# Splitting four halves of weights in a group's step, where eight were split

## The chip, the core and the metric

The kernel runs on one core of a Trainium2 chip. A core has a matrix engine (TensorE, PE in the rows, its weight loads PEld), VectorE (DVE), ScalarE (ACT), GpSimd (POOL) and SyncE (SP, which here only issues DMAs). Each engine works through its own list of instructions in the order of the program, and semaphores tell it when an input is there. The metric is the device time of one execution in microseconds (us), the median of several. Before the change it is 1352.58 us (three runs, 1352.49 to 1353.43).

## The reference

Three layers follow each other: a linear attention with gates, a feed-forward layer whose activation is a quotient of polynomials, and a mixture of four experts in which every token goes through every expert.

```
f = 1 / (1 + exp(-f_logit))
for t in range(S):                                   # S = 768, heads 8, batch 4, head size 48
    state = f[t, :, None] * state + outer(k[t], v[t])
    y[t] = q[t] @ state
x = y as 3072 tokens x 384
h = x @ w_in                                          # 384 -> 2048
g = (a0 + a1 h + a2 h^2 + a3 h^3) / (1 + |b0||h| + |b1| h^2 + 1e-6)
x = g @ w_out                                         # 2048 -> 384
for e in range(4):                                    # 384 -> 1024 -> 384
    out += p[:, e] * (relu(x @ w1[e]) @ w2[e])
```

## The kernel before

The 3072 tokens are six groups of 512 (four batches of 128 tokens). Three pipelines run over the groups at the same time and are woven into one list of steps, numbered v here and in the code (L1089): the attention of a later group, the first feed-forward layer of the next group, and the experts of the present group. `product_order` (L366) says which products a step holds. `in2` and `out2` are the two products of the experts for one slot of 128 hidden units, `in1` is the first product of the feed-forward layer, and `out1` is its second product for four slots at once. Products are computed from weights in two parts (a high part and the rest that it leaves), so `in1`, `in2` and `out2` are nine matmuls of 512 columns each and `out1` is 36. The steps 16, 20, 24 and 29 hold an `out1` and are called groups' steps.

A slot's weights are two halves (`halves`, L392). In the order of their use the halves are numbered k = 0, 1, 2, ... The first time that a half is used (96 of them, all within the steps -1 to 31) it goes through three stages. `make_ready` (L813) issues its load into one of NRAW = 8 places of a raw buffer. `split_to` (L832) splits it: ScalarE rounds it to the high part (L837, called a cast below) and GpSimd subtracts that from the raw values (L838, called a split). `store_all` sends both parts to memory, from where the later uses load them. A tile of the ring of R = 14 holds the two parts.

Who calls these sets the order of the engines' work. `take` (L847) gives a product its halves. After each product `emit` asks `make_ready` to load up to 14 halves ahead of the use. At a step's end (L1185) up to four halves are split, up to AHEAD = 8 ahead of the use. Where all eight raw places are taken, `make_ready` itself splits the oldest half until one is free (L822), in the middle of the step.

The other work that matters here, by line:

- `gate_in` and `gate_step`: the activation of the feed-forward layer. ScalarE copies the product (L947) and computes from it (L951, L952, L953, L968, L969, L978), VectorE multiplies (L962, L964 or L971, L967, L976, L986, L988, L993). One such unit is begun and one is finished in a step, and a step's L978 waits for its L976 and L969.
- `relu` (L1001 on ScalarE, L1002 on VectorE) empties the bank of an `in2`.
- `evac1`: after an `out1` its three banks are emptied, by ScalarE copies (L1058) in step 16 itself, by VectorE additions (L1060) in the steps 21, 25 and 29. `evac2` empties the banks of an expert (L1036 on VectorE, L1043 on GpSimd).
- the attention: GpSimd multiplies keys (L453) and queries (L468) by the gates' products, and TensorE's scores (L472) wait for the queries. L447 and L448 (ScalarE) and L459 and L463 (VectorE) make the factor of the queries; L426 is the exponential of the gates, whose logits are loaded as f. L492 and L548 (ScalarE), L553 and L567 (VectorE) and L568 (GpSimd) are the end of a block.

## Time and profile before

| | |
|---|---|
| median of three runs | 1352.58 us |
| profiled execution | 1352.66 us |
| its span, first to last instruction | 1350.9 us |
| TensorE busy | 1324.0 us, 98% |
| VectorE busy | 896.5 us, 66% |
| ScalarE busy | 666.5 us, 49% |
| GpSimd busy | 306.5 us, 23% |
| mean granted clock of TensorE | 0.995 |

The profiled execution is 1.8 us longer than its span. A row of the timeline gives the start in us from the span's start, the time from the first to the last of the merged instructions, the engine, the line, the operation, what it writes and reads, the number of instructions, and in brackets how long the engine sat idle before and what ended that. The granted clock is a share of TensorE's 2.4 GHz.

### The profile page before, as it was taken

Reading aid. Unit: us, or ns where it says so; the run is one execution under the profiler, and the core shown is the slowest. Engines: PE = TensorE matmul, PEld = TensorE weight load, DVE = VectorE, ACT = ScalarE, POOL = GpSimd, SP = SyncE. Lnnn points to the kernel's source line nnn. Section 1 sums busy time; section 2 is a strip of 40 time slices with the busy share of each in tenths; the row PEclk is TensorE's granted clock in tenths of the full one; section 3 lists DMA queues with packets and bytes.
Section 4 is the critical chain, followed back from the end, with each engine's and each line's share of the span. In section 5 each row is a group of like instructions: output and inputs, shape, how many; then the busy total and the mean of one; then the engine's idle time right before and its main releaser. Section 6 shows DMA issues by size and latency. Waiting matters only on the chain.

```text
span 1350.9 us, 19646 instructions
## 1 busy us (share of the span) xinstructions
PE 1324.0 (98%) x7180; PEld 1059.8 (78%) x7180; DVE 896.5 (66%) x1361; ACT 666.5 (49%) x1164; POOL 306.5 (23%) x263
## 2 busy tenths in 40 slices
PE   8998999999999999999999999999999999999998
PEld 7444888777788888888888888888888888888887
DVE  8999658998657666757666847676766465752221
ACT  5986458667344545445445525454535544531111
POOL 2334655676410122110120211010210010110010
PEclk9999999999999999999999999999999999999999
DMA  9537887677875676676666657665757666667660
GB/s 347 210 143 279 280 275 241 239 258 269 292 265 161 213 214 191 185 232 214 213 195 187 212 176 264 216 199 186 220 179 240 194 193 195 191 195 241 191 195 27
DMA packets 115705, 291.03 MB, mean 215 GB/s; under 512 B 13104, under 2 KB 28816, under 8 KB 114832
## 3 DMA queue, kind: packets, MB, share of 16 engines
q1 hardware_dynamic: 115168, 289.56, 66.6%
q8 instruction: 59, 0.97, 0.3%
q14 instruction: 46, 0.38, 0.1%
q10 hardware_dynamic: 432, 0.13, 0.0%
HBM read 240.83 MB, written 48.81 MB: 214 GB/s over the span
## 4 chain that ended last, share of the span: by engine, by line


## 5 line engine op out<-in xcount | busy, mean ns | idle before, releaser
L881 PE MATMUL bank<-x,w 128*128 128x512 f32 x2448 | 593.4, 391 | 3.1 <-DVE gl L1002 3.1
L881 PEld LDWEIGHTS bank<-x,w 128*128 128x128 f32 x2448 | 457.4, 188 | 99.7 <-DVE gl L1002 3.9
L891 PE MATMUL bank<-gh,w 128*128 128x512 f32 x1584 | 494.9, 394 | 3.6 <-DVE s L1060 2.6
L891 PEld LDWEIGHTS bank<-gh,w 128*128 128x128 f32 x1584 | 295.4, 189 | 69.7 <-ACT gh L978 4.4
L891 PE MATMUL bank<-gl,w 128*128 128x512 f32 x792 | 309.7, 391 | 0.0
L1002 DVE SCALAR_TENSOR_TENSOR gl<-bank,gh 128x512 fp32r<-128x512 f32 x192 | 131.5, 685 | 151.8 <-ACT gh L1001 151.5
L1043 POOL TENSOR_TENSOR o<-o,t 128x512 f32<-128x512 f32 x64 | 92.4, 1470 | 523.0 <-DVE t L1036 523.0
L1001 ACT ACTIVATE gh<-bank 128x512 fp32r<-128x512 f32 x192 | 113.9, 594 | 128.9 <-PE bank L881 128.9
L891 PEld LDWEIGHTS bank<-gl,w 128*128 128x128 f32 x792 | 149.4, 189 | 31.5
L967 DVE SCALAR_TENSOR_TENSOR q<-q,sc,r 128x512 f32<-128x512 f32 x80 | 64.8, 810 | 142.1 <-ACT r L952 142.1
L978 ACT CAST gh<-q 128x512 fp32r<-128x512 f32 x80 | 49.2, 615 | 162.9 <-DVE q L976 162.8
L838 POOL TENSOR_TENSOR w<-rawbuf,w 128x384 fp32r<-128x384 f32 x96 | 108.2, 1153 | 79.9 <-ACT w L837 64.3
L947 ACT COPY h<-bank 128x512 f32<-128x512 f32 x80 | 47.0, 588 | 113.6 <-PE bank L881 113.4
L993 DVE TENSOR_TENSOR gl<-q,gh 128x512 fp32r<-128x512 f32 x80 | 57.0, 713 | 32.8 <-ACT gh L978 32.6
L988 DVE SCALAR_TENSOR_TENSOR y<-y,sc,h 128x512 f32<-128x512 f32 x80 | 74.1, 927 | 2.8
L962 DVE SCALAR_TENSOR_TENSOR q<-q,r 128x512 f32<-128x512 f32 x80 | 72.6, 907 | 0.1
L968 ACT ACTIVATE r<-q,sc 128x512 f32<-128x512 f32 x80 | 58.0, 725 | 27.6 <-DVE q L967 20.5
L453 POOL TENSOR_TENSOR k<-k,g 112x512 f32<-112x512 f32 x23 | 34.1, 1484 | 144.7 <-DVE g L439 81.5
L953 ACT ACTIVATE y<-h,sc 128x512 f32<-128x512 f32 x80 | 64.1, 802 | 0.0
L976 DVE SCALAR_TENSOR_TENSOR q<-y,sc,q 128x512 f32<-128x512 f32 x80 | 62.2, 777 | 1.8
L969 ACT ACTIVATE r<-r 128x512 f32<-128x512 f32 x96 | 60.7, 632 | 3.0
L1060 DVE TENSOR_TENSOR s<-s,bank 128x512 f32<-128x512 f32 x45 | 30.0, 684 | 46.1 <-PE bank L891 46.0
(116 smaller groups left out, 1261.6 us busy)
## 6 DMA issues: line engine op xcount, KB each, us to landing
w<-ws SPq DMA_DIRECT2D x448, 384.0 KB, 3.6
ws<-w SPq DMA_DIRECT2D x96, 384.0 KB, 4.4
raw<-in_w_dram SPq DMA_DIRECT2D x16, 768.0 KB, 6.7
rawbuf<-in_w_dram SPq DMA_DIRECT2D x64, 192.0 KB, 4.2
v<-in_v_dram SPq DMA_DIRECT2D x24, 320.0 KB, 5.0
f<-in_qkf_dram SPq DMA_DIRECT2D x24, 256.0 KB, 3.6
k<-in_qkf_dram SPq DMA_DIRECT2D x24, 256.0 KB, 4.0
q<-in_qkf_dram SPq DMA_DIRECT2D x24, 256.0 KB, 4.3
```

The lines of the kernel that those rows point to most:

```text
L838: nc.gpsimd.tensor_tensor(out=t[:, 1], in0=r, in1=t[:, 0].bitcast(F32), op=ALU.subtract)
L881: nc.tensor.matmul(ps, a[:, o], b[:, kk, :], start=(n == 0), stop=(n == 8))
L891: nc.tensor.matmul(acc[m], a[:, o], b, start=(start and n == 0), stop=(stop and n == last))
L953: nc.scalar.activation(out=y, in_=h, func=AF.Identity, scale=sc[:, 0:1], bias=sc[:, 1:2])
L962: vec.scalar_tensor_tensor(out=q0, in0=q0, scalar=QC, in1=r0, op0=ALU.add, op1=ALU.mult)
L967: vec.scalar_tensor_tensor(out=q, in0=q, scalar=sc[:, 5:6], in1=r, op0=ALU.mult, op1=ALU.add)
L969: nc.scalar.activation(out=r, in_=r, func=AF.Exp, scale=-1.0)
L976: vec.scalar_tensor_tensor(out=q0, in0=y0, scalar=sc[:, 3:4], in1=q0, op0=ALU.subtract, op1=ALU.mult)
L988: vec.scalar_tensor_tensor(out=y, in0=y, scalar=sc[:, 2:3], in1=h, op0=ALU.subtract, op1=ALU.mult)
L1001: nc.scalar.activation(out=gh, in_=h, func=AF.Relu)
L1002: nc.vector.scalar_tensor_tensor(out=gl, in0=h, scalar=0.0, in1=gh.bitcast(F32), op0=ALU.max, op1=ALU.subtract)
L1043: add()
```

## The change

`make_ready` no longer splits a half to get room. Where the next half would need a raw place and all eight are taken, it stops, and the half is loaded later: a new call at each step's end, after the splits, goes on with the loads. `take` is made safe for a half that has not been loaded.

```
     def make_ready(n):
         while state["ready"] < min(n, len(uses)):
             k = state["ready"]
+            if first_use[k] and len(raw_of) >= NRAW:
+                break
             state["ready"] += 1
...
                     rawbuf.append(x2p.tile([128, NRAW, DM], F32, tag="x2", name="rawbuf"))
-                while len(raw_of) >= NRAW:
-                    split_to(state["split"] + 1)
                 r = raw_of[k] = rawbuf[0][:, len(seen) % NRAW]
...
     def take(n):
         k = state["used"]
-        split_to(k + n)
+        while state["split"] < k + n:
+            make_ready(state["split"] + 1)
+            split_to(state["split"] + 1)
         state["used"] += n
...
         if v >= -1:
             split_to(min(state["used"] + AHEAD, state["split"] + 4))
+            make_ready(state["used"] + R)
         att.loads(v)
```

The number of splits, their operands and all matmuls stay as they are; the lists of TensorE and of VectorE keep their order. What moves stands in the lists of ScalarE, GpSimd and SyncE. Counted from the code, the halves split in a step were 8 in each of the steps 16, 20 and 24, 2 in the steps 17, 21, 22 and 25, and 3 in the steps 18, 19, 23 and 26. They are now 4 in each of the steps 16 to 22 and 24 to 26, and 3 in the steps 23 and 27. In the steps -1 and 10 to 15 the number stays, but one split leaves the middle of the step for its end.

The first place is GpSimd at the steps -1 to 1. `w_1063`, `w_1065` and `w_1180` are the halves 6, 7 and 8, `k_1136` and `q_1138` the keys and queries of one block of the attention. Before:

```order
L468 TENSOR_TENSOR q_1073<-q_1073,i_1116 112x512
L838 TENSOR_TENSOR w_1063<-rawbuf_972,w_1063 128x384
L453 TENSOR_TENSOR k_1136<-k_1136,g_1153 112x512
L838 TENSOR_TENSOR w_1065<-rawbuf_972,w_1065 128x384
L838 TENSOR_TENSOR w_1180<-rawbuf_972,w_1180 128x384
L468 TENSOR_TENSOR q_1138<-q_1138,i_1199 112x512
```

And now:

```order
L468 TENSOR_TENSOR q_1073<-q_1073,i_1116 112x512
L453 TENSOR_TENSOR k_1136<-k_1136,g_1153 112x512
L838 TENSOR_TENSOR w_1063<-rawbuf_972,w_1063 128x384
L838 TENSOR_TENSOR w_1065<-rawbuf_972,w_1065 128x384
L838 TENSOR_TENSOR w_1180<-rawbuf_972,w_1180 128x384
L468 TENSOR_TENSOR q_1138<-q_1138,i_1195 112x512
```

The split of half 6 has moved behind the keys, so that three splits in a row stand ahead of the queries, where two stood. On ScalarE the cast of half 6 has moved behind L447, L448, L492 and L548 of the same step.

The second place is ScalarE in the steps 16 and 17. `w_2108` is half 46, the first that step 17 uses, and `s1` receives the banks of `out1`. Before:

```order
L978 CAST gh_2278<-q_2192 128x512
L837 CAST w_2108<-rawbuf_972 128x384
L1001 ACTIVATE gh_2321<-bank4_89 128x512
L837 CAST w_2144<-rawbuf_972 128x384
L837 CAST w_2155<-rawbuf_972 128x384
L837 CAST w_2183<-rawbuf_972 128x384
L837 CAST w_2220<-rawbuf_972 128x384
L837 CAST w_2231<-rawbuf_972 128x384
L1058 COPY s1_2391<-bank0_85 128x512
L1058 COPY s1_2391<-bank1_86 128x512
L1058 COPY s1_2391<-bank2_87 128x512
L837 CAST w_2256<-rawbuf_972 128x384
```

And now (lines behind `take` count two more: L1060 is L1058 of before, L1003 is L1001, L980 is L978):

```order
L980 CAST gh_2278<-q_2192 128x512
L1003 ACTIVATE gh_2317<-bank4_89 128x512
L1060 COPY s1_2367<-bank0_85 128x512
L1060 COPY s1_2367<-bank1_86 128x512
L1060 COPY s1_2367<-bank2_87 128x512
L837 CAST w_2108<-rawbuf_972 128x384
L837 CAST w_2144<-rawbuf_972 128x384
L837 CAST w_2165<-rawbuf_972 128x384
L837 CAST w_2183<-rawbuf_972 128x384
L949 COPY h_2393<-bank5_90 128x512
```

Six casts stood ahead of the copies and two behind; now four stand behind and none ahead, and `w_2108` is the first of them.

The third place is GpSimd in the steps 22 to 24, with `w_2769` as the first of its halves (half 70 now, 73 before). Before:

```order
L453 TENSOR_TENSOR k_2789<-k_2789,g_2848 112x512
L838 TENSOR_TENSOR w_2765<-rawbuf_972,w_2765 128x384
L838 TENSOR_TENSOR w_2769<-rawbuf_972,w_2769 128x384
L468 TENSOR_TENSOR q_2791<-q_2791,i_2894 112x512
L838 TENSOR_TENSOR w_2773<-rawbuf_972,w_2773 128x384
```

And now:

```order
L453 TENSOR_TENSOR k_2777<-k_2777,g_2828 112x512
L838 TENSOR_TENSOR w_2769<-rawbuf_972,w_2769 128x384
L838 TENSOR_TENSOR w_2771<-rawbuf_972,w_2771 128x384
L838 TENSOR_TENSOR w_2773<-rawbuf_972,w_2773 128x384
L838 TENSOR_TENSOR w_2775<-rawbuf_972,w_2775 128x384
L468 TENSOR_TENSOR q_2779<-q_2779,i_2886 112x512
```

Between the keys and the queries stand four splits, where two stood. In step 16 the same pair, `k_2167` and `q_2169`, had eight splits between them and now has four.

## Rows read from the trace of the kernel before

**Rows 1.** The page's busy time, share of the span and instructions, TensorE.
```profile
PE 1324.0 (98%) x7180; PEld 1059.8 (78%) x7180; DVE 896.5 (66%) x1361; ACT 666.5 (49%) x1164; POOL 306.5 (23%) x263
```

**Rows 2.** Waits of TensorE: line, releaser, us in total, times, longest.
```profile
PE bank L472 <- POOL q L468: 3.1, 2, 2.1
...
PE bank L891 <- DVE s L1060: 2.6, 1, 2.6
```

**Rows 3.** Busy time in a stretch: PE, PEld, DVE, ACT, POOL, clock, DMA share, GB/s.
```profile
362.40:1350.90 988.50, 981.92 (x5186) 812.49 (x5184) 593.29 (x901) 424.55 (x718) 118.80 (x95) 1.00 0.65 199
```

**Rows 4.** Timeline of step 1: casts and splits 7 and 8, queries, scores.
```profile
131.46 0.93 ACT L837 CAST w<-rawbuf 128x384 fp32r<-128x384 f32 x2
...
132.11 1.97 POOL L838 TENSOR_TENSOR w<-rawbuf,w 128x384 fp32r<-128x384 f32 x2 [1.85 <-issue]
...
134.05 1.27 POOL L468 TENSOR_TENSOR q<-q,i 112x512 f32<-112x512 f32 x1
...
135.37 1.16 PE L472 MATMUL bank<-q,k 48*128 48x128 f32 x16 [1.05 <-POOL q L468]
```

**Rows 5.** Busy time in four stretches after a wait of TensorE, columns as above.
```profile
252.70:256.00 3.30, 3.30 (x9) 2.61 (x8) 2.63 (x5) 3.27 (x7) 1.84 (x2) 0.50 1.03 414
286.90:290.10 3.20, 3.08 (x7) 2.48 (x8) 3.17 (x5) 1.29 (x3) 3.05 (x5) 0.50 0.86 219
...
345.10:348.40 3.30, 3.30 (x15) 2.73 (x16) 3.23 (x5) 0.84 (x2) 1.65 (x1) 1.00 1.04 395
350.90:354.20 3.30, 3.30 (x15) 2.71 (x16) 2.27 (x4) 0.00 (x0) 3.12 (x4) 1.00 0.93 302
```

**Rows 6.** Timeline of the steps 16 to 18.
```profile
241.22 8.30 POOL L838 TENSOR_TENSOR w<-rawbuf,w 128x384 fp32r<-128x384 f32 x8
241.23 7.42 DVE L962 SCALAR_TENSOR_TENSOR q<-q,r 128x512 f32<-128x512 f32 x1
...
242.61 0.62 PE L891 MATMUL bank<-gh,w 128*128 128x512 f32 x2
242.81 0.59 ACT L1058 COPY s<-bank 128x512 f32<-128x512 f32 x1 [2.13 <-PE bank L891]
...
245.28 0.71 ACT L952 ACTIVATE r<-h,sc 128x512 f32<-128x512 f32 x1
...
249.48 1.71 POOL L468 TENSOR_TENSOR q<-q,i 112x512 f32<-112x512 f32 x1
249.99 1.75 DVE L967 SCALAR_TENSOR_TENSOR q<-q,sc,r 128x512 f32<-128x512 f32 x1
...
251.24 1.16 PE L472 MATMUL bank<-q,k 48*128 48x128 f32 x16 [2.08 <-POOL q L468]
```

**Rows 7.** Timeline of the steps 20 to 22.
```profile
278.90 8.12 POOL L838 TENSOR_TENSOR w<-rawbuf,w 128x384 fp32r<-128x384 f32 x6
...
280.79 1.12 DVE L962 SCALAR_TENSOR_TENSOR q<-q,r 128x512 f32<-128x512 f32 x1
...
281.94 1.39 DVE L964 SCALAR_TENSOR_TENSOR q<-q,r 128x512 f32<-128x512 f32 x1
...
287.02 1.19 PE L891 MATMUL bank<-gh,w 128*128 128x512 f32 x2 [2.59 <-DVE s L1060]
...
293.29 0.67 DVE L962 SCALAR_TENSOR_TENSOR q<-q,r 128x512 f32<-128x512 f32 x1
```

**Rows 8.** Timeline of the steps 23 to 25.
```profile
301.74 1.74 POOL L468 TENSOR_TENSOR q<-q,i 112x512 f32<-112x512 f32 x1
...
305.02 1.16 PE L472 MATMUL bank<-q,k 48*128 48x128 f32 x16
...
321.66 0.70 PE L891 MATMUL bank<-gh,w 128*128 128x512 f32 x2 [0.98 <-ACT gh L978]
```

**Rows 9.** Timeline of the steps 25 to 29.
```profile
323.63 6.48 SPq L844 DMA_DIRECT2D ws<-w  x7
...
336.33 0.63 ACT L426 ACTIVATE f<-f 112x512 f32<-112x512 f32 x1 [1.70 <-DMA f<-in_qkf_dram]
...
345.05 2.33 PE L881 MATMUL bank<-x,w 128*128 128x512 f32 x9 [1.66 <-DVE gl L1002]
...
350.83 1.42 PE L881 MATMUL bank<-x,w 128*128 128x512 f32 x5 [1.41 <-DVE gl L1002]
```

More of the change, by code (lines that the diff above doesn't have):

```diff
@@ L815, in make_ready @@
             k = state["ready"]
+            if first_use[k] and len(raw_of) >= NRAW:
+                break
             state["ready"] += 1
@@ L821, in make_ready @@
                     rawbuf.append(x2p.tile([128, NRAW, DM], F32, tag="x2", name="rawbuf"))
-                while len(raw_of) >= NRAW:
-                    split_to(state["split"] + 1)
                 r = raw_of[k] = rawbuf[0][:, len(seen) % NRAW]
@@ L848, in take @@
         k = state["used"]
-        split_to(k + n)
+        while state["split"] < k + n:
+            make_ready(state["split"] + 1)
+            split_to(state["split"] + 1)
         state["used"] += n
@@ L1185, in fused @@
             split_to(min(state["used"] + AHEAD, state["split"] + 4))
+            make_ready(state["used"] + R)
         att.loads(v)
```

## The prediction

> **What bounds the kernel now.** I read the page's busy times first. TensorE works 1324.0 us of a span of 1350.9 us, VectorE 66% of it, ScalarE 49%, GpSimd 23% [rows 1]. The change touches no matmul, so it can move only the 27 us in which TensorE is idle, and what the clock loses after such idle times. The second view, busy times in stretches, says where they are not: from 362.40 us to the end TensorE is busy 981.92 of 988.50 us at full clock [rows 3], and no half is split behind step 31, which ends in this region. So I went with the third view, TensorE's waits, and with the timeline to the places before that at which TensorE waits for an engine that splits. There are six:
>
> - step 1, 1.05 us for the queries' product (L468) on GpSimd [rows 4];
> - step 18, 2.08 us for the same line [rows 6]. These two are the 3.1 us of [rows 2];
> - step 21, 2.59 us for an L1060 on VectorE, which stands behind VectorE's work on the gate units [rows 2, 7];
> - step 25, 0.98 us for an L978, the end of a gate unit [rows 8];
> - step 29, 1.66 and 1.41 us for L1002 on VectorE [rows 9].
>
> Together they are 9.77 us. The clock adds to this: in the stretches of 3.3 and 3.2 us after the waits of 2.08 and 2.59 us it was 0.50, and after those of 1.66 and 1.41 us it was 1.00 [rows 5]. The half-clock level is 1.2 GHz instead of 2.4, so each of the two stretches lost about 3.3 / 2 = 1.65 us of work.
>
> **Step 1.** The split of half 6 moves behind the keys, so three splits stand ahead of the queries' product where two did. GpSimd begins the two when ScalarE's casts at 131.46 us have given it the first high part, takes 1.97 us for them (0.98 each), and then multiplies the queries, for which TensorE waits [rows 4]. The cast of half 6 also moves behind L548 of that step, so the third split starts no earlier than the two did: it costs 0.98 us, nothing covers it (TensorE already waits there), and the wait becomes 1.05 + 0.98 = 2.03 us. That is nearly the 2.08 us after which the clock fell, and more than the 1.66 us after which it did not. I take the nearest row, so that 1.65 us come on top. Bounds: 0 (should half 6 be split while GpSimd waits for something else) and 0.98 + 1.65 = 2.63 us. I take 2.63. TensorE has no later slack here before step 18 to take this back.
>
> **Steps 16 to 18.** Two waits change places. The cast of `w_2108`, the first half that step 17 uses, now stands behind the L1058 copies. The last of these runs from 242.81 to 243.40 us; with one cast (0.93 / 2 = 0.46 us, [rows 4]) and one split (0.98) behind it the half is there at 243.40 + 0.46 + 0.98 = 244.84 us, and TensorE wants it at about 242.61 [rows 6]. That is a new wait of 2.2 us, and behind it in TensorE's list stands everything. In return the queries' product finds four splits ahead instead of the run of 8.30 us, so that the wait of 2.08 us goes. These two cancel within 0.2 us, with the half clock after either.
>
> **Steps 17 to 25.** What sets the waits in step 21 and 25 is the chain of the gate units through VectorE and ScalarE, and the splits disturb VectorE: one L962 took 7.42 us beside the run of eight splits, where another, with no split beside it, took 0.67 [rows 6, 7]. Three terms:
>
> - The starved L962 ends at 241.23 + 7.42 = 248.65 us, and L967 of its unit begins at 249.99. Not starved, L967 waits for L952, which ends at 245.28 + 0.71 = 245.99, and two more casts (0.93) now stand ahead of that unit on ScalarE: 246.92. Gain 3.07 us.
> - Steps 17 to 19 now split twelve halves where they split eight. A VectorE operation beside a split took 1.39 us instead of 0.67 [rows 7], 0.72 more. Four more splits cost 4 x 0.72 = 2.88 us.
> - In step 21 the splits no longer run beside L962 and L964, which took 1.12 and 1.39 us [rows 7]: (1.12 - 0.67) + (1.39 - 0.67) = 1.17 us gained.
>
> The chain so arrives 3.07 - 2.88 + 1.17 = 1.4 us earlier, and the wait in step 21 shrinks by so much. Then, in step 24, two more splits stand ahead of the queries' product. It ended at 301.74 + 1.74 = 303.48 us and TensorE wanted it at 305.02, without a wait [rows 8]: 1.54 us of cover. Two more splits take 1.97 us alone and 2 x 8.12 / 6 = 2.7 us beside VectorE's work [rows 4, 7], so 0.4 to 1.2 us of new wait, 0.8 in the middle. Net -0.6 us. Bounds: all of the waits of steps 21 and 25 with one half-clock stretch gone, -(2.59 + 0.98 + 1.65) = -5.2; and, if the first term gives nothing and step 24 costs its most, 2.88 - 1.17 + 1.2 = +2.9.
>
> The Trainium skill (SBUF — State Buffer, "Who interferes with whom") says that VectorE and GpSimd share one pair of ports and that an instruction takes it whole: a VectorE operation with two inputs in SBUF blocks while GpSimd holds it, in order of issue. The trace agrees with it for the L962 of 7.42 us and only in part for the one of 1.12, which lost less than one whole split. By the rule each added split would cost VectorE all of its 0.98 us, the second term would be 3.9 us and the whole sum 1.0 us higher; I go by the rows.
>
> **Steps 26 to 29.** Seven stores go through SP's queue in 6.48 us, and the load of f behind them makes ScalarE's L426 wait 1.70 us [rows 9]. The load now stands ahead of four of the stores, so that this wait goes. In its place one more cast (0.46) stands ahead and one more split beside VectorE's work (0.72): 1.70 - 0.46 - 0.72 = 0.52 us earlier, which comes off the waits of step 29. Bounds: 0 (L1002 is late for another reason) and -(1.66 + 1.41) = -3.07 us. I take -0.5. The other moved splits, steps 10 to 15, stand where TensorE does not wait for them; I cost them at nothing, and the cover is that each half is still split several halves ahead of its use. Loads that a step's end now issues were issued during the step before; a half that landed late would stall a cast by something like the 1.70 us of f, and I see no place where the eight raw places run dry.
>
> **Sum.** 2.63 + 0.1 - 0.6 - 0.5 = +1.6 us on the profiled execution's 1352.66 us, 1354.3; the median of the runs is 0.08 us below that execution, so 1354.2 us.
>
> **Rivals.**
>
> *The chain is freed (faster).* If splits in runs of four disturb VectorE less than the term of 0.72 us each says, because it finds gaps between them, the waits in step 21 and 25 go with the stretch at half clock behind the first: -5.2 us. For it speaks the 7.42 us, by far the largest disturbance in the trace, which no run of four can repeat; against it that the splits are as many as before. With the 0.98 us of step 1, the clock there not falling, and -0.5 in step 29 the time is 1352.58 + 0.98 - 5.2 - 0.5 = 1347.9 us; with step 29's waits gone too, 1345.3.
>
> *The queries come late (slower).* GpSimd's list is in order, and L468 is the one line there that TensorE waits for at once. If the chain gains nothing (0) and step 24's wait is at its 1.2 us, with a half-clock stretch behind it as in step 1, the sum is 2.63 + 0.1 + 1.2 + 1.65 - 0.5 = +5.1, 1357.7 us. It decides from where that wait gets beyond the 1.66 us after which the clock held; 1.2 is short of it, and only a chain that brings L468 itself late makes it so. For it speaks that in both waits of [rows 2] on this line splits stood ahead; against it that step 24 had 1.54 us of cover.
>
> *The change does not do what it says, or loads come too late.* The lists show the fours, so only the second half is open: a raw place freed at a step's end is loaded later than before, and a cast waits for its landing. Every such stall would be near 1.70 us; two of them beside the sum give 1357.6 us. In the trace nothing speaks for it.
>
> **How the numbers follow.** A measurement of this kernel can tell about 0.2% from no change, 2.7 us. The forecast, +1.6 us and so no change that can be told, gets 0.49; its own range is 1349.9 to 1355.3 us. The freed chain gets 0.27: the removal of the long run is certain, its worth is not. The late queries get 0.20 and the late loads 0.04, both slower. The range goes from 1346.3, most of the freed chain's cases, to 1358.0, where the loss bounds of step 1 and of the chain meet (2.63 + 2.9 = 5.5 us). Faster 0.27, same 0.49, slower 0.24.
>
> **What would show it.** Right: in step 1 three splits ahead of the queries and TensorE's wait for L468 near 2.0 us, with a clock of 0.5 behind it; a new wait of some 2.2 us in step 17 for a split; no wait for L468 in step 18; no L962 over 2 us; a wait of about 1.2 us (2.59 - 1.4) in step 21; a short one for L468 in step 24; L426 of step 27 without a wait for its load. Wrong: a clock of 1.0 after step 1's wait, no wait at all in step 21, or one in step 24 above 1.7 us; and any wait of a cast for a load.

## The result and the profile after: slower by 0.56%

The changed kernel takes 1361.02 us (median of six runs, 1359.14 to 1362.18), the kernel before 1352.80 (six runs, 1351.99 to 1353.54): a ratio of 1.0056, 95% interval 1.0045 to 1.0067. The forecast was 1354.2 us and the range ended at 1358.0, so the prediction was wrong: the loss is about 8.2 us where 1.6 were forecast. The span of the profiled execution grew by the same 8.3 us, from 1350.9 to 1359.2.

The page's busy times of the kernel after answer to [rows 1]:

```profile
PE 1327.3 (98%) x7180; PEld 1062.2 (78%) x7180; DVE 893.5 (66%) x1361; ACT 666.9 (49%) x1164; POOL 306.8 (23%) x263
```

They tell little. VectorE even has 3 us less to do. TensorE is busy 3.3 us longer with the same 7180 matmuls, so its clock will have to be looked at, and the other 5.0 us of the loss are idle time. TensorE's waits, the view of [rows 2], say more (line, releaser, us in total, times, longest):

```profile
PE bank L472 <- POOL q L468: 4.3, 3, 2.0
...
PE bank L883 <- DVE gl L1004: 3.7, 1, 3.7
PE bank L893 <- DVE s L1062: 3.4, 1, 3.4
...
PE bank L893 <- ACT w L837: 1.1, 1, 1.1
...
PE bank L893 <- POOL w L838: 0.6, 1, 0.6
```

Lines behind `take` count two more than before: L883 is the old L881, L893 the old L891, L980 the old L978, L1004 the old L1002, L1062 the old L1060. The two lines that were the long waits are still there, and longer.

TensorE's list did not change, so that the same matmul can be looked up in both traces. How late it starts, against [rows 4, 6 to 9], is the account of the loss:

| matmul that waits | before | after | later by |
|---|---|---|---|
| step 1, scores L472 | 135.37 | 135.84 | 0.5 |
| step 18, scores L472 | 251.24 | 253.54 | 2.3 |
| step 21, out2 behind L1062 | 287.02 | 289.85 | 2.8 |
| step 24, scores L472 | 305.02 | 310.01 | 5.0 |
| step 25, out2 | 321.66 | 327.12 | 5.5 |
| step 29, in2 behind L1004 | 345.05 | 352.50 | 7.5 |

Between these rows the delay changes as well: 2.1 us from the end of step 1 to step 15 (behind the half clock that follows the first row), 2.5 at the end of step 16, 4.6 behind the wait in step 17, 0.7 later in step 18 (the kernel before has its half clock there), 6.5 behind the half clock of step 24, and 8.1 at the end.

The rows behind the table, in the timeline of the kernel after. First step 1 and the steps 16 to 18:

```profile
131.62 2.94 POOL L838 TENSOR_TENSOR w<-rawbuf,w 128x384 fp32r<-128x384 f32 x3 [5.72 <-issue]
...
135.84 1.16 PE L472 MATMUL bank<-q,k 48*128 48x128 f32 x16 [1.74 <-POOL q L468]
...
245.27 0.59 ACT L1060 COPY s<-bank 128x512 f32<-128x512 f32 x1 [2.13 <-PE bank L893]
245.76 1.75 ACT L837 CAST w<-rawbuf 128x384 fp32r<-128x384 f32 x4
246.32 0.49 PE L893 MATMUL bank<-gh,w 128*128 128x512 f32 x1 [1.09 <-ACT w L837]
246.35 3.94 POOL L838 TENSOR_TENSOR w<-rawbuf,w 128x384 fp32r<-128x384 f32 x4 [2.46 <-ACT w L837]
247.41 0.50 PE L893 MATMUL bank<-gh,w 128*128 128x512 f32 x1 [0.59 <-POOL w L838]
...
253.54 1.16 PE L472 MATMUL bank<-q,k 48*128 48x128 f32 x16
```

Three splits stand ahead of the queries in step 1. In step 17 TensorE waits for the first half in two pieces, for its cast and then for its split, and in step 18 the scores wait for nothing. Then the four splits of step 17 (two before) beside VectorE's work on the units of step 18, and the three long waits that follow:

```profile
253.69 5.40 POOL L838 TENSOR_TENSOR w<-rawbuf,w 128x384 fp32r<-128x384 f32 x4 [1.70 <-ACT w L837]
253.84 1.50 DVE L995 TENSOR_TENSOR gl<-q,gh 128x512 fp32r<-128x512 f32 x1
...
256.81 1.39 DVE L966 SCALAR_TENSOR_TENSOR q<-q,r 128x512 f32<-128x512 f32 x1
258.13 1.50 DVE L969 SCALAR_TENSOR_TENSOR q<-q,sc,r 128x512 f32<-128x512 f32 x1
259.55 0.74 DVE L978 SCALAR_TENSOR_TENSOR q<-y,sc,q 128x512 f32<-128x512 f32 x1
...
289.85 0.70 PE L893 MATMUL bank<-gh,w 128*128 128x512 f32 x2 [3.41 <-DVE s L1062]
...
302.69 5.60 POOL L838 TENSOR_TENSOR w<-rawbuf,w 128x384 fp32r<-128x384 f32 x4 [4.87 <-ACT w L837]
...
310.01 1.16 PE L472 MATMUL bank<-q,k 48*128 48x128 f32 x16 [1.97 <-POOL q L468]
...
352.50 3.88 PE L883 MATMUL bank<-x,w 128*128 128x512 f32 x9 [3.74 <-DVE gl L1004]
```

While the four splits run, three of VectorE's five operations take 1.39 to 1.50 us (L1004 and L964, between the first and the second of them, take 0.69 and 0.79); the first behind the splits takes 0.74. Among VectorE's operations on gate units between 130 and 420 us, 27 took 1.2 to 2.0 us before and 38 do now, 18 and 29 of them beside a split; the one that took 7.42 us [rows 6] has no successor. So the change traded one operation that was held up by a whole run of eight splits for eleven that each wait for one split.

Busy times in stretches behind the waits, as in [rows 5] (PE, PEld, DVE, ACT, POOL, granted clock, DMA share, GB/s):

```profile
137.30:140.60 3.30, 3.30 (x9) 2.52 (x8) 2.77 (x4) 1.40 (x4) 2.72 (x3) 0.52 1.00 355
247.40:250.70 3.30, 3.29 (x14) 2.74 (x15) 1.40 (x1) 2.55 (x5) 3.30 (x4) 1.00 0.51 128
291.10:294.40 3.30, 3.30 (x9) 2.64 (x8) 3.26 (x4) 0.74 (x2) 3.30 (x3) 0.50 0.88 261
311.60:314.90 3.30, 3.30 (x9) 2.53 (x9) 2.24 (x4) 3.02 (x6) 2.07 (x3) 0.50 1.03 368
353.00:356.30 3.30, 3.30 (x10) 2.54 (x10) 3.22 (x6) 0.85 (x3) 1.19 (x1) 0.56 1.02 393
```

The clock fell to about its lower level (1.2 GHz) behind the waits of 1.74, 3.41, 1.97 and 3.74 us, and not behind the two pieces in step 17. In the kernel before it fell three times between the start and step 31: behind the waits of 2.08 and 2.59 us [rows 5], and once earlier, behind a wait of 2.65 us for VectorE at 118.48 us. The kernel after has the same wait of 2.65 us at 118.52 us, and the clock held. Before and after:

```profile
119.60:122.90 3.30, 3.30 (x7) 0.77 (x5) 3.12 (x6) 0.63 (x1) 1.27 (x1) 0.50 1.03 408
```

```profile
119.60:122.90 3.30, 2.74 (x21) 1.43 (x19) 3.12 (x6) 0.63 (x1) 1.27 (x1) 1.00 0.97 398
```

The net is one more fall, of some 1.6 us. A wait of a given length does not settle whether the clock falls. In a kernel further down (eight halves at a groups' step's end), whose lists up to step 1 are those of the kernel after, the wait in step 1 was as long and the clock held:

```profile
135.80 1.16 PE L472 MATMUL bank<-q,k 48*128 48x128 f32 x16 [1.75 <-POOL q L468]
...
137.30:140.60 3.30, 3.30 (x16) 2.74 (x15) 2.29 (x3) 2.05 (x4) 2.53 (x3) 1.00 1.00 363
```

So what is said below of single falls of the clock holds for the profiled execution.

### The profile page after: what moved, and what is told of

The parts are those of the page before. It is cut to its first block, busy times and chain, and to the rows that moved or that the text cites. A ratio compares the mean times of both kernels' runs of the same rounds, so it can differ in the third digit from the quotient of the medians.

```text
span 1359.2 us, 19655 instructions
## 1 busy us (share of the span) xinstructions
PE 1327.3 (98%) x7180; PEld 1062.2 (78%) x7180; DVE 893.5 (66%) x1361; ACT 666.9 (49%) x1164; POOL 306.8 (23%) x263
## 4 chain that ended last, share of the span: by engine, by line
## 5 line engine op out<-in xcount | busy, mean ns | idle before, releaser
L883 PE MATMUL bank<-x,w 128*128 128x512 f32 x2448 | 597.6, 393 | 4.3 <-DVE gl L1004 3.7
L883 PEld LDWEIGHTS bank<-x,w 128*128 128x128 f32 x2448 | 460.1, 189 | 102.3 <-DVE gl L1004 4.8
L893 PE MATMUL bank<-gh,w 128*128 128x512 f32 x1584 | 495.0, 394 | 5.2 <-DVE s L1062 3.4
L893 PEld LDWEIGHTS bank<-gh,w 128*128 128x128 f32 x1584 | 295.2, 188 | 72.2 <-ACT gh L980 3.8
L893 PE MATMUL bank<-gl,w 128*128 128x512 f32 x792 | 309.8, 391 | 0.0
L1004 DVE SCALAR_TENSOR_TENSOR gl<-bank,gh 128x512 fp32r<-128x512 f32 x192 | 131.4, 684 | 158.0 <-ACT gh L1003 157.7
L1003 ACT ACTIVATE gh<-bank 128x512 fp32r<-128x512 f32 x192 | 113.8, 593 | 127.9 <-PE bank L883 127.9
L893 PEld LDWEIGHTS bank<-gl,w 128*128 128x128 f32 x792 | 149.3, 189 | 31.3
L969 DVE SCALAR_TENSOR_TENSOR q<-q,sc,r 128x512 f32<-128x512 f32 x80 | 67.0, 837 | 143.7 <-ACT r L954 143.7
L980 ACT CAST gh<-q 128x512 fp32r<-128x512 f32 x80 | 49.2, 615 | 161.6 <-DVE q L978 161.4
L838 POOL TENSOR_TENSOR w<-rawbuf,w 128x384 fp32r<-128x384 f32 x96 | 109.2, 1166 | 77.8 <-ACT w L837 68.9
L964 DVE SCALAR_TENSOR_TENSOR q<-q,r 128x512 f32<-128x512 f32 x80 | 66.9, 836 | 0.1
L978 DVE SCALAR_TENSOR_TENSOR q<-y,sc,q 128x512 f32<-128x512 f32 x80 | 64.6, 807 | 1.8
L1062 DVE TENSOR_TENSOR s<-s,bank 128x512 f32<-128x512 f32 x45 | 30.0, 683 | 47.2 <-PE bank L893 47.2
```

Of the source, the lines that this page charges most:

```text
L838: nc.gpsimd.tensor_tensor(out=t[:, 1], in0=r, in1=t[:, 0].bitcast(F32), op=ALU.subtract)
L883: nc.tensor.matmul(ps, a[:, o], b[:, kk, :], start=(n == 0), stop=(n == 8))
L893: nc.tensor.matmul(acc[m], a[:, o], b, start=(start and n == 0), stop=(stop and n == last))
L964: vec.scalar_tensor_tensor(out=q0, in0=q0, scalar=QC, in1=r0, op0=ALU.add, op1=ALU.mult)
L969: vec.scalar_tensor_tensor(out=q, in0=q, scalar=sc[:, 5:6], in1=r, op0=ALU.mult, op1=ALU.add)
L978: vec.scalar_tensor_tensor(out=q0, in0=y0, scalar=sc[:, 3:4], in1=q0, op0=ALU.subtract, op1=ALU.mult)
```

## The experiments

A ratio is that of the kernel's runs to those of the kernel before on the same chip, with its 95% interval. Differences from the changed kernel's 1361.02 us are differences of medians from several chips; the difference of the ratios (1.0056 for the changed kernel) stands beside them where it tells something else. The intervals reach 0.1 to 0.15% to either side, some 1.5 to 2 us. The theories are named in the expectations. What theory A stands for: the change took splits out of the groups' steps and put them into the steps between, where ScalarE and VectorE pass each gate unit round in a loop (cast L980, VectorE's L964, L966, L969, L978, and again L980) that takes longer than TensorE's work.

**The queries ahead of the splits.** Edit of the changed kernel:

```
-            return {..., DVE1: [blk.newton1], REST: [blk.newton2]}
+            return {..., DVE1: [blk.newton1], REST: [blk.newton2, blk.q_hat]}
         if k == 3:
-            return {POOL1: [blk.q_hat]}
+            return {}
```

> The changed kernel, with the queries' product (L468) of a block issued at the end of the step before, right behind the factor that it needs and so ahead of that step's splits. Theory A (splits taken out of the groups' steps and put into the steps between, where each costs about 1.1 us: a cast on ScalarE and a VectorE operation slowed beside the split; in addition queries behind more splits): the waits for L468 of 1.74 us (step 1) and 1.97 us (step 24) go, with the half-clock stretches behind them (about 1.65 us each), the rest of the loss stays: 1361.0 - 1.7 - 2.0 - 3.3 = 1354 us, or up to 1357 where the gate units' chain takes some back. Rival B (loads and splits at a step's end come too late as such, for whoever waits): another wait takes their place and the time stays within 2 us of 1361.

Measured: 1359.41 us, ratio 1.0057 (1.0043 to 1.0071): by the medians 1.6 us less than the changed kernel, by the ratios no gain. Both waits for L468 of 1.74 and 1.97 us are gone (0.7 us of waiting is left in step 1), but behind the scores of step 24, which no longer wait, another wait stands, for VectorE:

```profile
301.41 4.03 DVE L964 SCALAR_TENSOR_TENSOR q<-q,r 128x512 f32<-128x512 f32 x1
...
301.93 4.38 POOL L838 TENSOR_TENSOR w<-rawbuf,w 128x384 fp32r<-128x384 f32 x4
...
304.41 1.16 PE L472 MATMUL bank<-q,k 48*128 48x128 f32 x16
...
310.80 0.50 PE L883 MATMUL bank<-x,w 128*128 128x512 f32 x1 [2.96 <-DVE gl L1004]
```

Theory A's number was missed, and rival B's was met. But most of the new wait was made by the edit. With the queries ahead of them the four splits ran without a gap and held up one L964 for 4.03 us: from the start of L964 to the end of L978 VectorE needed 6.23 us, against 3.84 in the same place of the changed kernel, where L964 took 1.00. That is 2.4 of the 2.96 us. So this run does not tell what the queries' wait in step 24 alone was worth, and no more than some 0.6 us of the new wait can be the lateness that the gate units' loop already had.

**Eight halves in a groups' step again, at its end.** Edit of the changed kernel:

```
-            split_to(min(state["used"] + AHEAD, state["split"] + 4))
+            split_to(min(state["used"] + AHEAD, state["split"] + (8 if v in groups else 4)))
```

> The changed kernel, with up to eight halves split at the end of a group's step instead of four. The halves per step are then 8, 2, 3, 3 again as before the change, but all at the step's end. Theory A: the steps 18 to 20 take no longer than before, the wait in step 21 goes back to about 2.6 us or less and those of step 24 (1.97 us and half clock) and step 29 (3.74 us) go back as well; left are step 1 (+1.9 us) and the wait for the first half in step 17: 1353 to 1356 us. Rival B (it is the place at the end of the step, with loads issued there): 1360 to 1362 us, as the change has it.

Measured: 1355.42 us, ratio 1.0030 (1.0018 to 1.0043). By the medians the distribution of the halves over the steps alone is worth 5.6 us of the loss, by the ratios 3.5; in the profiled execution 1.6 us of the gain are the clock of step 1, which this edit does not touch. Rival B falls. Theory A's number is met, its reason only in part: the steps 18 to 20, measured as in the table below, took 24.61 us, hardly less than in the changed kernel, since the eight splits begin behind the copies and run into step 18. The wait in step 21 fell to 1.5 us, and step 24 has none for L468.

**GpSimd writes and reads nothing.** Edit, once of the changed kernel and once of the kernel before:

```
-                nc.gpsimd.tensor_tensor(out=t[:, 1], in0=r, in1=t[:, 0].bitcast(F32), op=ALU.subtract)
+                nc.gpsimd.memset(t[:, 1].bitcast(F32), 0.0)
```

> The changed kernel, with GpSimd writing zeros in place of the low part of a half, so that it reads nothing; it leaves out the low parts of the weights. The casts stay. Theory A, port term: VectorE's L966, L969 and L978 beside the splits fall from about 1.4 to about 0.7 us, 0.7 us for each moved split, and the waits for L468 shrink with the shorter GpSimd work: some 4 to 6 us less than the changed kernel, 1355 to 1357 us. Rival C (the loss is in the casts' order on ScalarE alone): the operations are shorter but the waits in the steps 21 and 29 stay, 1359 to 1361 us. To be read against the same edit of the kernel before.

> The kernel before, with the same edit: GpSimd writes zeros in place of the low part of a half, which leaves out the low parts of the weights. The L962 of 7.42 us goes and with it the waits of 2.08, 2.59 and 0.98 us in part: 1345 to 1350 us. Theory A: the difference between the two kernels shrinks from 8.2 us to what the casts cost and the first half's wait in step 17, 2 to 4 us. Rival C: the difference stays at 7 to 8 us.

Measured: 1341.59 us (0.9921, 0.9908 to 0.9935) and 1339.69 us (0.9909, 0.9894 to 0.9924). Both gain far more than I expected, and the difference between the two kernels shrinks from 8.2 to 1.9 us. The groups by line in the changed kernel and in this one (out<-in xcount, busy, mean ns, idle before; L966 between 130 and 420 us):

```profile
L966 DVE SCALAR_TENSOR_TENSOR q<-q,r 128x512 f32<-128x512 f32 x17 | 18.9, 1114 | 0.6
```

```profile
L966 DVE SCALAR_TENSOR_TENSOR q<-q,r 128x512 f32<-128x512 f32 x17 | 12.0, 704 | 0.6
...
L838 POOL MEMSET w<- 128x384 f32 x96 | 36.1, 419 | 16.7 <-DMA ws<-w 8.1 <-PE bank L893 4.9 <-ACT r L971 1.6
```

With no reading on GpSimd's side, L966 takes 704 ns as if alone. The edit also makes GpSimd's own work shorter (419 ns instead of 1166), so the queries come earlier too; it does not separate that from VectorE's slowing. The next two dose casts and splits apart. The dose of splits makes GpSimd's list longer as well, so that the loop has to be read by itself, in the table behind them.

**Twelve casts twice, and twelve splits twice.** Both are edits of the kernel before, whose groups' steps keep their eight halves:

```
+            twice[0] = {17: 2, 18: 1, 19: 1, 21: 2, 22: 2, 25: 2, 26: 1, 27: 1}.get(v, 0)
             split_to(min(state["used"] + AHEAD, state["split"] + 4))
+            twice[0] = 0
...
-                nc.scalar.copy(out=t[:, 0], in_=r)
+                for _ in range(1 + (twice[0] > 0)):
+                    nc.scalar.copy(out=t[:, 0], in_=r)
+                twice[0] -= 1
```

and for the second kernel the same loop about the subtraction on GpSimd instead of the copy.

> The kernel before, in which twelve casts are done twice: 2 in step 17, 1 in 18, 1 in 19, 2 in 21, 2 in 22, 2 in 25, 1 in 26, 1 in 27. These are the steps, and the numbers, in which the change adds halves; the groups' steps keep their eight. ScalarE works 0.41 us longer for each. Theory A1 (the price of a moved half is the slowed VectorE operation beside its split): within 1.5 us of 1352.1. Theory A2 (it is the cast in ScalarE's part of the loop): 4 to 6 us slower.

> The kernel before, in which twelve splits on GpSimd are done twice, in the same steps and numbers; the casts are single. Theory A1: each second split slows a VectorE operation by 0.7 us in a step whose length VectorE and ScalarE set: 4 to 8 us slower, with waits in the steps 21, 25 and 29 like those of the changed kernel. Theory A2: within 2 us of 1352.1.

Measured: casts 1355.15 us, ratio 1.0018 (1.0009 to 1.0026), some 2.4 us; splits 1360.20 us, ratio 1.0055 (1.0042 to 1.0069), 7.4 us. The dose of splits alone brings nearly the whole loss, with the same waits as in the changed kernel:

```profile
PE bank L472 <- POOL q L468: 5.1, 4, 2.1
PE bank L883 <- DVE gl L1004: 3.5, 1, 3.5
PE bank L893 <- DVE s L1062: 3.0, 1, 3.0
```

The number for the splits is theory A1's (4 to 8 us). That for the casts is neither's: A1 had said at most 1.5 us, A2 4 to 6. So the casts have a share, smaller than A2 claimed. The waits for L468 also grew, from 3.1 us in all to 5.1, which is GpSimd's lateness and not VectorE's. How much of each there is in the loop can be read from the start of the gh cast (ScalarE) at the steps' ends. In the kernel before, at the end of step 17 and of step 20:

```profile
253.06 0.60 ACT L978 CAST gh<-q 128x512 fp32r<-128x512 f32 x1
...
274.23 0.60 ACT L978 CAST gh<-q 128x512 fp32r<-128x512 f32 x1
```

and after:

```profile
252.57 0.62 ACT L980 CAST gh<-q 128x512 fp32r<-128x512 f32 x1 [0.31 <-DVE q L978]
...
277.90 0.60 ACT L980 CAST gh<-q 128x512 fp32r<-128x512 f32 x1
```

| kernel | steps 18, 19, 20 together | against its base |
|---|---|---|
| before | 21.17 us | |
| after (four more halves in 17 to 19) | 25.33 us | +4.16 |
| before, four casts twice | 22.64 us | +1.47 |
| before, four splits twice | 24.25 us | +3.08 |
| before, GpSimd not reading | 19.59 us | |
| after, GpSimd not reading | 21.17 us | +1.58 |

A moved half costs this stretch 1.04 us (4.16 / 4): by the doses 0.37 us for its cast and 0.77 for its split, which is a little more than 1.04 together, and without reading on GpSimd the casts are what is left, 0.4 us each.

**The queries early in the kernel before,** the edit of the first experiment:

> The kernel before, with the queries' product (L468) issued at the end of the step before, ahead of the splits. The changed kernel with this edit was 1.6 us faster than without it, since its wait in step 24 was taken over by one for the gate units. Theory A (VectorE beside splits sets the waits of the steps 21, 25 and 29): of the waits for L468, 1.05 us and 2.08 us with half clock, the first goes for good and the second is taken back in step 21: 1350 to 1352 us. Rival (the queries are what is late): 1352.1 - 1.05 - 2.08 - 1.65 = 1347 us.

Measured: 1352.96 us, ratio 0.9999 (0.9990 to 1.0008). Nothing is gained: both waits for L468 go, and others take their place, for ScalarE's L947 in step 18 and for L1002 in step 24. The number lay just above theory A's.

**The splits on VectorE:** in the kernel before all from half 46 on, then only those of the steps after 16 that hold no `out1`, then the latter in the changed kernel:

```
-                nc.gpsimd.tensor_tensor(out=t[:, 1], in0=r, ...)
+                (nc.vector if k >= 46 else nc.gpsimd).tensor_tensor(out=t[:, 1], in0=r, ...)
...
+                (nc.vector if v > 16 and v not in groups else nc.gpsimd).tensor_tensor(out=t[:, 1], in0=r, ...)
```

> The kernel before, with the splits of half 46 and all later ones on VectorE instead of GpSimd, so that no split stands beside a VectorE operation from step 16 on, and each costs VectorE its own time, about 0.5 us, in place of 0.7 us of slowing; none stands ahead of the queries on GpSimd. Theory A: the waits of the steps 18, 21, 25 and 29 shrink: 1342 to 1349 us. Rival (VectorE's list, with eight splits in a row in a group's step, becomes late for the copies out of the banks): 1352 us or more.

> The kernel before, with the splits of the steps after 16 on VectorE, except those of the groups' steps, which stay on GpSimd. Theory A1 (a split on GpSimd costs the steps between 0.7 us each by the VectorE operation that it slows, and nothing beside an out1): the steps 17 to 20 are some 4 us shorter in sum, as with all splits on VectorE, and the groups' steps don't pay for eight splits in VectorE's own list as they did there: 1344 to 1350 us. Rival (the list of VectorE is the limit, whoever splits): 1352 to 1357 us.

> The changed kernel with the same edit. Theory A1: each of the moved halves costs VectorE about 0.5 us of its own in place of the slowing, and the queries of step 24 stand behind no split: 1350 to 1356 us, at least 5 us less than the changed kernel. Rival (order of the casts or of the loads): 1359 to 1362 us.

Measured: 1356.37 us, ratio 1.0026 (1.0015 to 1.0036); 1355.48 us, 1.0023 (1.0013 to 1.0033); 1358.56 us, 1.0045 (1.0031 to 1.0058). The first two missed theory A's numbers and met the rival's, the third gained 2.5 us against the changed kernel (1.5 by the ratios) where at least 5 were expected. A split on VectorE takes

```profile
L838 DVE TENSOR_TENSOR w<-rawbuf,w 128x384 fp32r<-128x384 f32 x50 | 29.8, 638 | 12.0 <-ACT w L837 11.8
```

638 ns in the mean, and VectorE stood idle for 12.0 us before these 50, 11.8 of them for the casts, 0.24 us for each. Together that is no less than the 0.7 us of slowing that it replaces.

**Both gaining edits in one kernel:** eight halves at the end of a groups' step, and the queries ahead of the splits.

> The changed kernel with both edits that gained: up to eight halves split at the end of a group's step, and the queries' product ahead of the splits of the step before. Theory A: from 1355.4 us with the eight alone, the step 1 part goes (about 2.7 us) and the wait of 3.1 us for L468 in step 18 with its half clock, which part of step 21's wait takes back: 1349 to 1352.5 us. Rival (what is left is the first half of step 17, cast behind the copies): 1353 us or more.

Measured: 1354.50 us, ratio 1.0014 (1.0005 to 1.0023); the rival's number. No version that computes the whole reference beat the kernel before.

**Half 6 split early again.** Edit of the changed kernel, by which only the first forced split comes back:

```
             if first_use[k] and len(raw_of) >= NRAW:
-                break
+                if state["split"] > 6:
+                    break
+                split_to(state["split"] + 1)
```

> The changed kernel with the first place undone: one split is forced in step -1, as before the change, so that half 6 is split ahead of the keys again; all later steps as changed. Both theories: the wait in step 1 goes back to about 1.05 us and the half clock behind it goes: 2 to 3 us less than the changed kernel, 1358 to 1359 us, if nothing later takes it back; 1360 to 1362 us if it does.

Measured: 1358.46 us, ratio 1.0045 (1.0032 to 1.0059), 2.6 us less than the changed kernel (1.5 by the ratios). In the timeline of this kernel the scores wait as before the change, and the clock behind them does not fall, though it held behind 1.75 us as well, as shown above:

```profile
135.11 1.16 PE L472 MATMUL bank<-q,k 48*128 48x128 f32 x16 [1.04 <-POOL q L468]
```

and the busy times behind it (columns as above):

```profile
135.50:138.80 3.30, 3.30 (x25) 2.75 (x24) 3.20 (x5) 0.76 (x2) 3.15 (x5) 1.00 1.01 339
```

**This and the eight halves together:**

> The changed kernel with both places undone: one split forced in step -1, and up to eight halves split at the end of a group's step; left of the change are the place at the step's end and the loads there. If the two parts add up as each did alone (2.6 and 5.6 us of the 8.5): 1352 to 1353.5 us. If something of the change is left that neither shows: 1354 to 1357 us.

Measured: 1355.34 us, ratio 1.0019 (1.0010 to 1.0028). By the medians they gain no more together than the eight halves alone (1355.42), by the ratios 1.5 us more. Against the kernel before 0.19% are left: something of the change is left. In the trace it is step 17 and 18: a wait of 1.09 us for the cast of the first half, and one of 3.1 us for L468, since all eight splits now begin behind the copies out of the banks.

**Twelve splits twice in the groups' steps** of the changed kernel, the dose of above at the other place:

```
+            twice[0] = 4 * (v in (16, 20, 24))
             split_to(min(state["used"] + AHEAD, state["split"] + 4))
+            twice[0] = 0
```

> The changed kernel, in which the four splits of the steps 16, 20 and 24 are done twice on GpSimd: twelve more, the same dose that made the kernel before 7.4 us slower when it was given in the steps between. Theory A1 (the place decides: beside a group's out1 a split costs little, in the steps between it costs the loop of VectorE and ScalarE): 0 to 2.5 us slower than the changed kernel, 1361 to 1363.5 us. Rival D (the number of splits decides, wherever they stand): 6 to 9 us slower, 1367 to 1370 us.

Measured: 1366.13 us, ratio 1.0098 (1.0081 to 1.0114), 5.1 us above the changed kernel and between the two theories. The timeline shows two reasons. The splits of step 16 stand behind the copies and so behind its `out1`: they run from 245.88 us, beside the work of step 17, and the dose makes TensorE wait for the first half's second subtraction (1.66 us, where it was 0.59) and for the queries (2.01, where it was nothing):

```profile
248.00 0.50 PE L895 MATMUL bank<-gh,w 128*128 128x512 f32 x1 [1.66 <-POOL w L839]
...
257.85 1.16 PE L472 MATMUL bank<-q,k 48*128 48x128 f32 x16 [2.01 <-POOL q L468]
```

And VectorE is held up:

```profile
256.71 4.51 DVE L968 SCALAR_TENSOR_TENSOR q<-q,r 128x512 f32<-128x512 f32 x1
...
257.76 4.33 POOL L839 TENSOR_TENSOR w<-rawbuf,w 128x384 fp32r<-128x384 f32 x4
```

and once more at 305.63 us, for 4.57 us. With GpSimd late, four splits run without a gap, and one VectorE operation is held up by all of them, in a step between. So this run does not settle whether the place of a split or the number of splits sets the price: of the three doses only that of step 24 stood beside its `out1` (that of step 20 began at 288.74 us, where the `out1` ran from 282.19 to 290.51), and a longer run pushes the next splits onto other operations. That a split beside an `out1` costs little is not shown by any run.

**Each split as two instructions** of 192 columns, in the kernel before and in the changed one:

```
+                for o in (slice(0, DM // 2), slice(DM // 2, DM)):
+                    nc.gpsimd.tensor_tensor(out=t[:, 1, o], in0=r[:, o], in1=t[:, 0, o].bitcast(F32), op=ALU.subtract)
```

> The kernel before, with each split on GpSimd done as two instructions of 192 columns. If a VectorE operation beside a split waits for one whole instruction of GpSimd (alternating, 1.4 us instead of 0.7), it now waits for half as much, about 0.35 us: the steps 18 to 29 get shorter and the time falls by 1 to 4 us, to 1349 to 1352 us. If GpSimd's time decides, whatever its pieces, or its longer work (about 0.2 us more for each split) brings the queries later: 1352 to 1356 us.

> The changed kernel with the same edit, which has some eleven more alternating operations than the kernel before and none that was held up for a whole run of splits. If the price goes by the length of GpSimd's instruction: 4 to 6 us less than the changed kernel, 1355 to 1357 us. If by GpSimd's time: 1360 to 1364 us.

Measured: 1357.64 us, ratio 1.0035 (1.0022 to 1.0047), above both ranges, and 1363.29 us, 1.0079 (1.0065 to 1.0092), in the second. Shorter instructions did what the first theory said to the operations that take turns, and the time did not fall. In the changed kernel with this edit such an operation takes 1.0 to 1.15 us instead of 1.4 to 1.5, and one is held up by a whole run:

```profile
249.61 1.08 DVE L979 SCALAR_TENSOR_TENSOR q<-y,sc,q 128x512 f32<-128x512 f32 x1
...
251.74 5.55 DVE L991 SCALAR_TENSOR_TENSOR y<-y,sc,h 128x512 f32<-128x512 f32 x1
...
252.82 4.94 POOL L839 TENSOR_TENSOR w<-rawbuf,w 128x192 fp32r<-128x192 f32 x8
```

Of VectorE's operations on gate units between 130 and 420 us, 45 took 0.95 to 1.2 us there (3 in the changed kernel) and 7 took 1.2 to 2.0 (38). What stands against that gain is two hold-ups, of 5.55 and 7.27 us, where the changed kernel has none (10.72 instead of 7.42 us in the kernel before with the edit), and GpSimd's time for the 96 halves, which rose from 109.2 to 134.3 us. Which of the two weighs more is not shown.

## Why the prediction was wrong

- **Step 1: the wait right, the clock by luck.** The forecast was 2.63 us, 0.98 from the third split and 1.65 from the clock. The wait grew to 1.74 us instead of 2.03, and with the half clock behind it TensorE was 2.1 us late. But the fall of the clock belongs to the execution: where it held behind the same wait, TensorE was 0.4 us late (the changed kernel with the eight halves) or 1.1 us (the one with splits on VectorE). Undoing this place alone gave 2.6 us back by the medians, 1.5 by the ratios.
- **Steps 16 to 18: the waits right, the clock not.** The new wait for the first half came, 1.09 and 0.59 us, and put TensorE 2.1 us later there (forecast 2.2); the one for the queries went. The clock stayed at 1.00 behind the new wait, where half clock was assumed behind either, so that some 1.6 us were gained. This too belongs to the execution: in the kernel with half 6 split early the clock behind the same wait was 0.50, from 246.0 to 249.0 us. The next steps took the gain back.
- **Steps 17 to 25: the step that failed.** "The chain so arrives 3.07 - 2.88 + 1.17 = 1.4 us earlier, and the wait in step 21 shrinks by so much." The first term was about right: the gh cast of step 17 came 0.5 us earlier although TensorE was 2.3 us late by then, so 2.8 us were gained. The second was too small. Four moved halves cost the next three steps 4.16 us, not 2.88: the cast of each, 0.4 us, stands in the same loop on ScalarE ahead of the copy of the next unit, and I had priced only VectorE's part, at 0.72 (0.77 by the dose). The third term was right but for its size (step 21 gave back 0.84 us of 1.17). So the wait in step 21 grew from 2.59 to 3.41 us.
- **Step 24:** the forecast was 0.8 us of wait at full clock; it was 1.97 us at half clock. Two splits stood ahead of the queries in the kernel before, from 299.03 us and for 2.75 us (row below); now it is the four at 302.69 us that take 5.60. Two more cost 2.85 us, as priced (2.7), which is 1.3 beyond the cover of 1.54. The other 0.6 us is the loop: the splits began 3.7 us later than before, while TensorE wanted the scores only 3.0 us later. The bound of 1.2 us had counted the splits alone. A wait above 1.7 us here was one of the prediction's own signs of being wrong.

```profile
299.03 2.75 POOL L838 TENSOR_TENSOR w<-rawbuf,w 128x384 fp32r<-128x384 f32 x2 [3.90 <-PE bank L881]
```

- **Steps 26 to 29: the other failure.** "In its place one more cast (0.46) stands ahead and one more split beside VectorE's work (0.72)." The wait of L426 for its load went, as forecast. But of the twelve halves that the change moves, I priced four in the steps 17 to 19, two in step 24 and one here. The ones moved into the steps 21, 25 and 27 had no price at all. The wait in step 29 went from 1.66 and 1.41 us to 3.74 us with half clock behind it. That these halves did it, at about 1.1 us each, is argued from the steps 18 to 20, and no run doses them alone; the trace shows the four splits of step 26 beside VectorE operations of 1.39 to 1.50 us:

```profile
341.97 5.28 POOL L838 TENSOR_TENSOR w<-rawbuf,w 128x384 fp32r<-128x384 f32 x4
...
346.30 1.50 DVE L978 SCALAR_TENSOR_TENSOR q<-y,sc,q 128x512 f32<-128x512 f32 x1
```

- **The rivals.** The slower rival named the queries on GpSimd as the mechanism. Its condition came true in step 24: the chain brought L468 itself late, and the wait got beyond 1.66 us. But it is not the main part by what the runs show: with the queries moved out of the way in both places 1.6 us of the 8.2 were saved by the medians and nothing by the ratios, in a run that got a hold-up of its own. The late loads did not come: the casts waited 1.9 us in all for loads, 2.4 before. The distribution of the halves, 3.5 to 5.6 us, was no rival of mine.
- **The Trainium skill** (SBUF — State Buffer, "Who interferes with whom") says that a VectorE operation with two inputs in SBUF contends with a GpSimd instruction that reads SBUF and not with one that only writes it. The trace agrees: L966 takes 1114 ns in the mean in the kernel whose GpSimd subtracts, 704 where it writes. I had cited the section for its price of a single split and gone by the rows; by the page the sum would have been 1.0 us higher and still far too low, because the count was wrong and not only the price. That the trace agreed with the page for the 7.42 us was too much said: a rule for one instruction gives a hold-up of one split, 0.98 us, and not of a run of eight.

What stays open: what each place was worth. Step 1 and the distribution gave back 2.6 and 5.6 us by the medians and 5.7 together; by the ratios it is 1.5, 3.5 and 5.0. With 1.5 us or more of noise in each the runs don't tell whether the parts add up. The doses of splits and casts came to 9.8 us, more than the loss. Each part ends in waits that the next one hides, and in clock falls that come with some of them.

## What to carry to other kernels

When a change spreads a burst of work evenly, first find what the burst stood beside. Eight splits in a row, begun 1.4 us before a long product ended, held up one VectorE operation for 7.42 us, of which only about 3 reached the loop; the same splits in the steps between cost about 1 us apiece. Price every moved instruction, on each engine that it passes, in the step where it lands, and count that they add up to all that are moved, before weighing any single wait. And look in an experiment's trace for what the edit itself has made before its time is read as the price of what it removed.

## What the runs showed of the hardware

- VectorE and GpSimd met in two ways. Either they took turns, and a VectorE operation beside a split mostly took 1.4 to 1.5 us instead of 0.7; or one VectorE operation stood until a whole run of GpSimd's was through, 7.42 us for eight splits, 4.51 for four. With GpSimd's instructions half as long, taking turns cost less (1.0 to 1.15 us for most), and the hold-ups got longer: 10.72 us in the kernel before with that edit.
- The subtractions on GpSimd, by what they read and by their length, cost the kernel before about 12.5 us in all: 1352.14 against 1339.69 us where GpSimd only wrote. No order of the same splits gained anything like it.
- Equal waits of TensorE were followed by different clocks: behind 2.65 us at 118.5 us the clock was 0.50 in the kernel before and 1.00 in the kernel after, behind 1.74 and 1.75 us in step 1 about 0.5 and 1.00.
- Where the waits for the queries were removed, others stood on other lines: for L1004 in step 24 of the changed kernel, most of it made by the edit, and for L947 (3.0 us) and L1002 (1.8 us) in the kernel before.
